# A retention layer and a snake MLP on one core: another written-out order for the first three blocks

## The chip, the cores and the metric

The kernel runs on one core of a Trainium2 chip. The metric is the device time of one execution in microseconds; the times shown are medians of several runs.

## What is computed

The reference, cut to what matters:

```
scores = scale * q @ k.T                              # q, k, v: (8 batches, 8 heads, 576, 64)
ret    = scores * D      # D[i,j] = gamma_h ** (i-j) for i >= j, else 0
x      = (ret @ v), heads side by side                # (4608, 512)
h      = x @ w_in                                     # (512, 2048)
s      = sin(alpha * h)
g      = h + s * s / (alpha + 1e-9)
out    = g @ w_out                                    # (2048, 512) -> (4608, 512) float32
```

Everything comes as float32; the kernel rounds the operands of the matmuls to float16.

## The kernel before

**Tiling.** The 4608 rows are worked as nine blocks of 512 rows. Blocks 0 to 7 are the first 512 rows of each batch; block 8 is the last 64 rows of all eight batches together. In a batch, the 512 rows are two pieces `p` of 256 rows, and the retention is computed in chunks of 128 rows with a carried state `kvs` instead of the full triangle.

**Attention of a batch, `at[b]`.** `load(b, nm, p)` brings one piece of q, k or v as 512 KB on SP's DMA queue into a `raw` buffer (six of them). `cast` scales it by powers of gamma and rounds it to float16, on the engine named: `V` is VectorE (DVE in the profile), `A_` is ScalarE (ACT), `G_` is GpSimd (POOL); `(0,)` or `(1,)` is one half. The transposed form comes from `turn` (eight matmuls on TensorE into a PSUM bank) followed by `take` (a copy out of the bank), or later in the kernel from `crossed` (a transposing DMA on SP's queue). `outer` makes the products of k and v for the state, `take_sum`, `next_sum`, `evict` and `more` bring them out and add them up, `to_state` scales and rounds the state, `scores` and `masked` make `ret`, `values` and `add_states` make the output of the attention, and `keep` copies it as float16 into `xT`.

**The MLP of a block.** `project(n, fc)` is four matmuls of 128x512 that make one of the 16 column groups of `h` in a PSUM bank (with a last argument 0 or 1, only for the first or second 256 rows). `sine` is on ScalarE, `square` on the engine named, `product` on VectorE adds the two and writes `gT`; it is also what gives the PSUM bank back. `gemm2(n, u)` is four matmuls for a quarter of one of the four output tiles, `finish(n, c)` copies the tile out and stores it. The banks have the names `h0`, `h1`, `h2`, `op` (one bank each) and `m0`, `m1` (two banks each).

**Weights.** `load_w_in(g)` and `load_w_out(g)` bring a quarter of each matrix, 1 MB of float32 written as 512 KB of float16, on GpSimd's DMA queue.

**Order.** All work of blocks 0 to 2, with the attention of batches 0 to 4 that goes with it, is written out by hand, one call a line (lines 637 to 1113): each engine executes its instructions in the order of that list, and semaphores come from the tiles that the calls share. From block 3 on (line 1117) a loop over 16 units a block gives the order. `keep_busy` issues matmuls on zeros, so that TensorE has work while data comes. A tile with `bufs=n` goes round n buffers in the order of the requests.

Of the kernel before, what the change touches and what calls it, by code (L numbers as in the profile page):

```python
# [10 lines left out]
F32 = mybir.dt.float32  # L11
F16 = mybir.dt.float16
ADD = mybir.AluOpType.add
MULT = mybir.AluOpType.mult


@with_exitstack
def kernel(
# [86 lines left out]

    raw = {}
# [3 lines left out]
    def load(b, nm, p):  # L110
        if p < 2 and b >= HALVED and nm != "q":
            t_ = work.tile([P, H, 2 * D], F32, tag="raw", bufs=6, name=nm + "32")
# [6 lines left out]
        elif p < 2:  # L119
            t_ = work.tile([P, H, 2 * D], F32, tag="raw", bufs=6, name=nm + "32")  # L120
# [10 lines left out]
    nbuf = {"k": 4, "q": 3, "v": 4}  # L131

    def cast(b, nm, p, eng, ys=(0, 1)):
        t_ = raw[b, nm, p]
        if (b, nm, p) not in half:
            if p < 2:
                d_ = work.tile([P, 16 * D], F16, tag=nm + "16", bufs=nbuf[nm], name=nm + "16")
# [41 lines left out]
    def new_T(b, nm, p):  # L179
        if (b, nm, p) not in T:  # L180
            T[b, nm, p] = (
                work.tile([P, 8, P], F16, tag=nm + "T", bufs=4, name=nm + "T")
                if p < 2
                else work.tile([P, 4, P], F16, tag=nm + "Ts", bufs=B // 2, name=nm + "Ts")
            )
        return T[b, nm, p]
# [54 lines left out]
    class Attention:  # L241
# [11 lines left out]
        def tile(self, name, shape, dtype, bufs):  # L253
            if name not in self.tiles:
                self.tiles[name] = work.tile(shape, dtype, tag=name, bufs=bufs, name=name)
            return self.tiles[name]

        @property
        def x(self):
            xs[self.b] = self.tile("xT", [P, KT, 512], F16, 3)  # L260
            return xs[self.b]

        @property
        def kvs(self):
            return self.tile("kvs", [P, 4, 4, D], F32, 1)

        def state_of(self, c):
            return self.tile("s16", [P, 3, 4, D], F16, 2)[:, c] if c < 3 else sS[:, self.b]
# [56 lines left out]
        def more(self, c):  # L325

            s32 = work.tile([P, 4, D], F32, tag="s32", bufs=2, name="s32")
# [27 lines left out]
        def masked(self, p, y):  # L355
            sc = self.sc.pop((p, y))
            ret = work.tile([P, 2, 512], F16, tag="ret", bufs=4, name="ret")
# [171 lines left out]
    def sine(n, fc):  # L529
        hps = hps_of[n, fc][0]  # L530
        s_t = work.tile([P, 512], F16, tag="s", bufs=4, name="s_t")
# [5 lines left out]
    def square(n, fc, eng):  # L537
        s_t = hps_of[n, fc][1]
        ss_t = work.tile([P, 512], F16, tag="ss", bufs=4, name="ss_t")
# [56 lines left out]

    def make_constants():
# [30 lines left out]
    with tc.manual_schedule():  # L628
# [7 lines left out]

        load(0, "k", 0)
        load(0, "q", 0)
        cast(0, "q", 0, V, (1,))
        cast(0, "k", 0, V, (1,))  # L640
        cast(0, "k", 0, G_, (0,))
        load(0, "v", 0)
        cast(0, "v", 0, A_)
        keep_busy(16, "h0", 256)
        keep_busy(44, "op", 64)
        at[0].outer((0,), "h0", "h1")
        cast(0, "q", 0, V, (0,))
        turn(0, "k", 0, "op")
        turn(0, "q", 0, "h2")
        take(0, "k", 0, V, (0,))  # L650
        at[0].take_sum(0, V)
        take(0, "k", 0, A_, (1,))
        take(0, "q", 0, A_)
        load(0, "q", 1)
        cast(0, "q", 1, G_)
        load_w_in(0)
        load(0, "k", 1)
        cast(0, "k", 1, V)
        load_w_in(2)
        turn(0, "q", 1, "h0")  # L660
        at[0].scores(0, 1, "m0")
        turn(0, "k", 1, "h1")
        at[0].to_state(0, A_)
        take(0, "k", 1, A_)
        load(0, "v", 1)
        at[0].scores(0, 0, "m1")
        turn_alpha()
        take_alpha()
        keep_busy(10, "h2", 256)
        take(0, "q", 1, A_)  # L670
        load(1, "q", 1)
        at[0].take_sum(1, V)
        at[0].more(1)
        at[0].to_state(1, A_)
        cast(0, "v", 1, V)
        at[0].masked(0, 1)
        at[0].masked(0, 0)
        load_w_in(1)
        at[0].outer((1,), "h2", "h1")
        cast(1, "q", 1, G_)  # L680
        at[0].scores(1, 0, "m0")
        turn(1, "q", 1, "op")
        at[0].masked(1, 0)
        at[0].scores(1, 1, "m1")
        at[0].masked(1, 1)
        at[0].take_sum(2, A_)
        at[0].more(2)
        load_w_in(3)
        at[0].to_state(2, G_)
        load_w_out(0)  # L690
# [3 lines left out]
        at[0].values(1, False, "h0", "h2")  # L694
        load(1, "q", 0)
        take(1, "q", 1, A_)
        at[0].values(1, True)
        at[0].add_states(1)
        at[0].keep(0, V)
        project(0, 2, "m1", 0)  # L700
        at[0].keep(1, V, A_)
        project(0, 2, "m1", 1)
        sine(0, 2)
        project(0, 1, "op")
        keep_busy(2, "h0")
        square(0, 2, V)
        invert_alpha()
        product(0, 2)
        cast(1, "q", 0, G_)
        load(1, "v", 0)  # L710
        at[0].next_sum(3)
        sine(0, 1)
        square(0, 1, A_)
        project(0, 0, "h2")
        sine(0, 0)
        cast(1, "v", 0, A_)
        project(0, 8, "h0", 0)
        project(0, 3, "m0")
        sine(0, 3)
        project(0, 8, "h0", 1)  # L720
        product(0, 1)
        square(0, 0, V)
        product(0, 0)
        square(0, 3, G_)
        product(0, 3)
        project(0, 11, "m1")
        load_w_out(1)
        sine(0, 8)
        turn(1, "q", 0, "op")
        take(1, "q", 0, A_, (0,))  # L730
        sine(0, 11)
        take(1, "q", 0, V, (1,))
        project(0, 6, "h1")
        sine(0, 6)
        square(0, 6, V)
        at[0].to_state(3, G_)
        load_w_out(2)
        square(0, 11, A_)
        product(0, 6)
        product(0, 11)  # L740
        project(0, 7, "h2")
# [494 lines left out]
```

## Time and profile before

| | |
|---|---|
| median of 3 runs | 307.27 us (306.55 to 307.67) |
| profiled execution | 306.96 us |
| its span, first to last instruction | 305.2 us |
| mean granted TensorE clock | 0.994 |
| busy: TensorE / VectorE / ScalarE / GpSimd | 293.5 / 204.5 / 182.7 / 136.2 us |
| first `project` (block 0) starts | 20.91 us |
| first `project` of block 1 starts | 50.26 us |
| first `gemm2` of the loop (block 3's stage) | 107.74 us |

In the profile's rows a group is one line of the kernel on one engine; after the count comes the busy time and, in brackets or behind a bar, how long the engine stood idle before it and what it waited for. PEld is the weight load, which runs beside PE. The page's busy time of PE is not a measure of PE at its peak, since matmuls overlap; the distance from one matmul to the next is.

### The profile page before, as it was taken

Reading aid. Unit: us, or ns where it says so; the run is one execution under the profiler, and the core shown is the slowest. Engines: PE = TensorE matmul, PEld = TensorE weight load, DVE = VectorE, ACT = ScalarE, POOL = GpSimd, SP = SyncE. Lnnn points to the kernel's source line nnn. Section 1 sums busy time; section 2 is a strip of 40 time slices with the busy share of each in tenths; the row PEclk is TensorE's granted clock in tenths of the full one; section 3 lists DMA queues with packets and bytes.
Section 4 is the critical chain, followed back from the end, with each engine's and each line's share of the span. In section 5 each row is a group of like instructions: output and inputs, shape, how many; then the busy total and the mean of one; then the engine's idle time right before and its main releaser. Section 6 shows DMA issues by size and latency. Waiting matters only on the chain.

```text
span 305.2 us, 7933 instructions
## 1 busy us (share of the span) xinstructions
PE 293.5 (96%) x3257; PEld 149.6 (49%) x3257; DVE 204.5 (67%) x296; ACT 182.7 (60%) x294; POOL 136.2 (45%) x155
## 2 busy tenths in 40 slices
PE   6879989999999999999999999999999999999995
PEld 5655556455444544454445444544454454444443
DVE  2768988899679796767665777566666746555600
ACT  1649935675365758665677567756764556555411
POOL 4794760498379488578039726653030000000000
PEclk9799999999999999999999999999999999999999
DMA  8999999997695978978689989866441111111132
GB/s 232 338 217 216 216 247 330 242 312 188 166 256 167 167 175 199 255 124 181 146 226 178 170 190 257 161 143 161 105 112 37 34 37 37 35 35 37 46 88 72
DMA packets 115508, 49.85 MB, mean 163 GB/s; under 512 B 69760, under 2 KB 110992, under 8 KB 115472
## 3 DMA queue, kind: packets, MB, share of 16 engines
q1 hardware_dynamic: 110912, 44.97, 62.8%
q0 software_dynamic: 4224, 4.19, 8.1%
q8 instruction: 25, 0.41, 0.6%
q10 hardware_dynamic: 336, 0.18, 0.3%
q14 instruction: 11, 0.09, 0.1%
HBM read 36.75 MB, written 9.44 MB: 151 GB/s over the span
## 4 chain that ended last, share of the span: by engine, by line
PE 82%; DMA 9%; POOL 3%; DVE 2%; ACT 1%; SPq 1%; issue 1%; DVEq 0%; ACTq 0%
PE ops L567 39%; PE hps L524 36%; DMA v<-in_v_dram 7%; PE sc L347 2%; PE o L389 2%; DMA q<-in_q_dram 2%; PE kv L283 1%; POOL q L169 1%; SPq L121 1%; POOL w_in L92 1%; PE o L411 1%; DVE ss_t L543 1%; DVE k L169 0%; DVE ret L359 0%; ACT v L102 0%
## 5 line engine op out<-in xcount | busy, mean ns | idle before, releaser
L567 PE MATMUL ops<-w_out,gT 128*128 128x512 f16 (+2 forms) x592 | 142.4, 373 | 0.9 <-DMA w_out<-in_moe_w_out_dram 0.4
L548 DVE SCALAR_TENSOR_TENSOR gT<-ss_t,inva,hps 128x512 f16<-128x512 f16 x144 | 106.2, 745 | 52.0 <-ACT ss_t L541 45.5
L532 ACT ACTIVATE s_t<-hps,alpha_t 128x512 f16<-128x512 f32 x144 | 97.3, 687 | 70.9 <-PE hps L524 68.1
L524 PE MATMUL hps<-xT,w_in 128*128 128x512 f16 (+1 forms) x544 | 126.5, 367 | 0.3
L524 PEld LDWEIGHTS <-w_in 128*128 128x128 f16 x608 | 58.6, 98 | 64.5 <-DVE xT L104 0.6
L567 PEld LDWEIGHTS <-gT 128*128 128x128 f16 x592 | 56.3, 98 | 65.0 <-issue 1.6
L543 DVE TENSOR_TENSOR ss_t<-s_t 128x512 f16<-128x512 f16 x72 | 43.6, 608 | 19.3 <-ACT s_t L532 18.7
L541 ACT ACTIVATE ss_t<-s_t 128x512 f16<-128x512 f16 x62 | 38.8, 632 | 0.9
L102 ACT COPY osb<-ops 128x512 f32<-128x512 f32 (+1 forms) x34 | 19.7, 582 | 22.0 <-PE ops L567 20.6
L169 POOL TENSOR_TENSOR k<-k,cn 128x1024 f16<-128x1024 f32 (+1 forms) x13 | 22.3, 1712 | 22.1 <-DMA k<-in_k_dram 17.9
L169 POOL TENSOR_TENSOR q<-q,cn 128x1024 f16<-128x1024 f32 (+1 forms) x16 | 27.2, 1710 | 10.9 <-DMA q<-in_q_dram 10.9
L359 DVE TENSOR_TENSOR ret<-sc,mask 128x1024 f16<-128x1024 f32 x20 | 23.9, 1219 | 4.2 <-PE sc L347 4.2
L329 POOL TENSOR_TENSOR kvs<-s,kvs 128x256 f32<-128x256 f32 x22 | 16.2, 734 | 4.0 <-ACT kvs L102 2.3
L543 POOL TENSOR_TENSOR ss_t<-s_t 128x512 f16<-128x512 f16 x10 | 10.8, 1084 | 14.6 <-ACT s_t L532 14.6
L102 ACT CAST xT<-o 128x1024 f16<-128x1024 f32 (+1 forms) x14 | 13.2, 957 | 6.1 <-PE o L411 5.9
L524 PE MATMUL hps<-xS,w_in 128*128 128x512 f16 x64 | 16.4, 379 | 0.0
L153 POOL TENSOR_TENSOR ks<-ks,cn 128x512 f16<-128x512 f32 x4 | 4.2, 1044 | 24.6 <-DMA vs<-in_v_dram 18.1
L104 POOL CAST v<-v 128x1024 f16<-128x1024 f32 (+1 forms) x10 | 10.0, 1007 | 11.1 <-DMA v<-in_v_dram 11.1
L328 POOL TENSOR_TENSOR s<-kvs,cn 128x256 f32<-128x256 f32 x22 | 14.3, 650 | 0.3
L321 POOL TENSOR_TENSOR s<-kvs,cn 128x256 f16<-128x256 f32 x19 | 12.2, 646 | 0.9 <-ACT kvs L102 0.4
L389 PE MATMUL o<-ret,v 64*64 64x128 f16 (+1 forms) x512 | 11.0, 214 | 0.9 <-DVE ret L359 0.4
L359 DVE TENSOR_TENSOR ret<-sc,mask_halved 128x768 f16<-128x768 f32 x12 | 11.4, 950 | 0.0
(62 smaller groups left out, 148.9 us busy)
## 6 DMA issues: line engine op xcount, KB each, us to landing
out_dram<-osb SPq DMA_DIRECT2D x70, 128.0 KB, 2.8
q<-in_q_dram SPq DMA_DIRECT2D x16, 512.0 KB, 5.4
k<-in_k_dram SPq DMA_DIRECT2D x10, 512.0 KB, 5.6
v<-in_v_dram SPq DMA_DIRECT2D x10, 512.0 KB, 6.4
k<-in_k_dram SPq DMA_DIRECT2D x24, 128.0 KB, 3.1
v<-in_v_dram SPq DMA_DIRECT2D x24, 128.0 KB, 3.3
w_in<-in_moe_w_in_dram POOLq DMA_DIRECT2D x4, 512.0 KB, 11.6
w_out<-in_moe_w_out_dram POOLq DMA_DIRECT2D x4, 512.0 KB, 11.5
```

What stands on the lines that cost most here:

```text
L102: eng.copy(d_, s_)
L169: eng.tensor_tensor(dst[:, a0:a1].rearrange("p a r t d -> p t (a r) d"), t_.rearrange("p (t a) x -> p t a x", t=2)[:, :, a0:a1].rearrange( ...
L328: nc.gpsimd.tensor_tensor(s32, self.kvs[:, c - 1], g1.unsqueeze(2).to_broadcast([P, 4, D]), MULT)
L329: nc.gpsimd.tensor_tensor(self.kvs[:, c], s32, self.kvs[:, c], ADD)
L359: nc.vector.tensor_tensor(ret.rearrange("p t (z x) -> p (t z) x", z=2)[:, :, 0:n], sc.rearrange("p t (z x) -> p (t z) x", z=2)[:, :, 0:n], ...
L389: made.append(matmul(o[t][halves(e), c : c + 128].rearrange("p (r i) -> p r i", r=2)[:, :, i0:64], v16[halves(g), 4 * t + 2 * x + e, r, :] ...
L524: matmul(hps_of[n, fc][0][:, cols], w_in16[:, a, fc * P : (fc + 1) * P], xs[n][:, a, cols], start=(a == 0 and part != 1), stop=(a == KT - ...
L532: nc.scalar.activation(s_t, hps, mybir.ActivationFunctionType.Sin, bias=0.0, scale=alpha_t[:, fc : fc + 1],)
L541: nc.scalar.activation(ss_t, s_t, mybir.ActivationFunctionType.Square)
L543: eng.tensor_tensor(ss_t, s_t, s_t, MULT)
L548: nc.vector.scalar_tensor_tensor(gT[n][:, fc, :], ss_t, inva[:, fc : fc + 1], hps, MULT, ADD)
L567: matmul(ops[n, c, cols.start][:, cols], gT[n][:, fk, c * P : (c + 1) * P], w_out16[:, fk, cols], start=(fk == 0), stop=(fk == FC - 1), sk ...
```

## The change

Three things change; what is computed stays the same.

1. The written-out list for blocks 0 to 2 is replaced as a whole. The same loads, projections, second matmuls and attention steps are in it, in another order, with other engines and PSUM banks. Counted in the two lists: squares on VectorE 20 before and 12 after, on ScalarE 18 and 25, on GpSimd 10 and 11; casts (a half counts as one) on VectorE 15 and 9, on GpSimd 21 and 26, on ScalarE 5 and 5. `wait_for_w_out(g)`, a small DMA on SP's queue that reads a quarter of `w_out` and so holds that queue until the quarter is there, is called four times; the function was there before and was not called.
2. Which SBUF buffer a tile gets comes from a table, `BUFFERS`, one digit for each request, and no longer from going round.
3. In the last stage four more small DMAs, `fill_up`, are put on SP's queue.

In the loop, the banks of the projections go round as `h2, h1, h0` where they went `h2, h0, h1`.

```diff
+BUFFERS = {
+    "raw": "012345024135024135043250130124130254103254103254",
+    "k16": "0123012310230123",
+    "q16": "0121021010210210",
+    "v16": "0123012310320132",
...
+}
...
+    def place(tag, shape, dtype):
+        name = tag + next(slot_of[tag])
+        if name not in places:
+            places[name] = work.tile(shape, dtype, tag=name, bufs=1, name=name)
+        return places[name]
...
-            t_ = work.tile([P, H, 2 * D], F32, tag="raw", bufs=6, name=nm + "32")
+            t_ = place("raw", [P, H, 2 * D], F32)
...
+    PAD = 4
+
+    def fill_up():
+        nc.sync.dma_start(gate, w_out16[:, 0, 0:64])
...
-        h, m = cycle(("h2", "h0", "h1")), cycle(("m0", "m1"))
+        h, m = cycle(("h2", "h1", "h0")), cycle(("m0", "m1"))
...
             if n == 7:
+                for i in range(PAD):
+                    at_unit(3 + i, fill_up)
```

The new list from its start to the first projections, one call after the other:

```
load k0; cast k0 V(0), V(1); turn k0 h0; take k0 A_(1), V(0); load q0, v0; cast v0 A_(0)
keep_busy 3 op, 3 h1; load q1; cast q1 V(0); cast v0 G_(1); keep_busy 1 op; outer(0) h1,h2
load k1; cast k1 V; cast q0 G_; turn q0 h0; take q0 A_; take_sum(0) V; next_sum(1)
load_w_in(0); cast q1 G_(1); load v1; load (1,q,0); cast v1 A_; cast (1,q,0) V
turn k1 op; turn q1 h0; take q1 A_; take k1 A_; scores(0,1); outer(1); take_sum(2) A_
to_state(0) G_; load_w_in(2); more(2); masked(0,1); scores(0,0); masked(0,0); load_w_in(1)
turn (1,q,0) h0; take A_; scores(1,1) m0; keep_busy(21, h1, 128); to_state(2) G_; masked(1,1)
scores(1,0); turn_alpha; take_alpha; to_state(1) A_; masked(1,0); take_sum(3) A_
values(0) m0; keep(0) A_; values(1) h1,h0; load (1,q,1); cast (1,q,1) G_; keep(1) A_,V
turn (1,q,1) op; take V(0); load_w_in(3); project(0,2); take A_(1); project 0, 3, 11, 8, 1, 7, 6, 9, 5, ...
```

(`k0` is piece 0 of k of batch 0; `(1,q,1)` is piece 1 of q of batch 1.) In the old list `(1,q,1)` is loaded, cast and turned there too, and `(1,q,0)` is turned among the projections of block 0. Further down, the new list has

```
square(0,2) G_; product; square(0,0) G_; load_w_out(1); ... square(0,11) G_; ... load_w_out(0), load_w_out(2)
... more(3) of batch 0; load_w_out(3); ... project(0,12) op, (0,14) h0, (0,13) m1, (0,15) h2, (0,4) m0, (0,10) h1
take (1,k,0) A_(1); sine(0,10); cast (1,v,0) A_(1); square(0,10) A_; take (1,k,0) A_(0); gemm2(0,4), (0,12), (0,5), (0,13)
wait_for_w_out(0); scores, outer(0) of batch 1; ... gemm2(0,14), (0,6), (0,7); scores(1,1); load (1,v,1); cast (1,v,1) A_; outer(1)
... gemm2(0,15), (0,0), (0,1); values; gemm2(0,2), (0,3); project(1,6), (1,3), (1,9), (1,7), ...
```

so that twelve `gemm2` of block 0 stand ahead of the first `project` of block 1, where the old list has nine; the other four follow later.

More of the change, by code (lines that the diff above doesn't have):

```diff
@@ L679 @@
[L679 to L682, printed above, removed]
-        at[0].masked(1, 0)
[L684 to L690, printed above, removed]
+        at[0].to_state(1, A_)
+        at[0].masked(1, 0)
+        at[0].take_sum(3, A_)
         at[0].values(0, False, "m0")
@@ new lines @@
+        product(1, 0)
+        cast(3, "k", 0, G_)
+        at[2].to_state(3, G_)
+        load(4, "q", 0)
+        crossed(3, 1, "k")
+        load(4, "k", 0)
+        crossed(3, 0, "q")
+        load(4, "v", 1)
+        crossed(3, 0, "k")
+        at[2].scores(0, 0, "m0")
+        at[2].scores(0, 1, "m1")
+        at[2].masked(0, 1)
+        sine(1, 2)
+        square(1, 2, A_)
+        product(1, 2)
+        at[2].masked(0, 0)
+        project(1, 1, "h1")
+        sine(1, 1)
+        gemm2(0, 11, "h0")
@@ L977 @@
[L977 to L988 removed]
+        cast(3, "v", 1, G_)
+        gemm2(1, 0, "h2")
+        gemm2(1, 1, "h2")
+        gemm2(1, 2, "h2")
+        gemm2(1, 3, "h2")
+        load(4, "k", 1)
+        at[3].scores(1, 0, "m0")
```

773 lines of the change are left out of this document (385 added, 388 removed).

## The prediction

> **What bounds the kernel now.** I read the page's first lines, then the busy times by stage, then PE's part of the chain of waits.
>
> ```profile
> PE 293.5 (96%) x3257; PEld 149.6 (49%) x3257; DVE 204.5 (67%) x296; ACT 182.7 (60%) x294; POOL 136.2 (45%) x155
> ...
> 50.30:106.90 56.60, 56.08 (x734) 28.66 (x733) 47.62 (x65) 34.39 (x56) 37.13 (x39) 1.00 0.93 220
> 36.70:50.30 13.60, 12.17 (x262) 6.70 (x261) 12.20 (x21) 6.02 (x12) 7.19 (x9) 1.00 1.17 272
> 20.90:36.70 15.80, 15.69 (x99) 8.79 (x99) 12.74 (x26) 14.35 (x23) 9.43 (x10) 1.00 1.19 216
> 0.00:20.90 20.90, 14.86 (x327) 12.04 (x328) 11.02 (x16) 9.22 (x19) 14.59 (x24) 0.92 1.04 266
> ...
> 92.61 5.18 PE ops L567 x24
> ```
>
> A stage row gives its length, then the busy time of PE, PEld, DVE, ACT, POOL, then clock, DMA share and GB/s. PE is the bound from 20.9 us on. 5.18 us over 24 matmuls is 0.216 us each, so a `project` or `gemm2` of four is 0.863. Whatever DVE, ACT and POOL save is worth nothing unless PE was waiting, and PE's waits are few: 0.1 us idle in the first 15.8, 1.4 in the next 13.6, 0.5 in the 56.6. The loop's first second matmul starts at 107.74 (below), and what is behind it hardly changes. So the change can win at most about 2 us after 20.9 us, plus what it does to the first 20.9 us. There it can also lose.
>
> **The change part by part.** First the head: when does the first projection start?
>
> ```profile
> 7.82 1.04 ACT L102 CAST v<-v 128x1024 f16<-128x1024 f32 x1 [4.55 <-DMA v<-in_v_dram]
> ...
> 9.36 1.90 POOL L169 TENSOR_TENSOR q<-q,cn 128x1024 f16<-128x1024 f32 x1 [3.40 <-DMA q<-in_q_dram]
> ...
> 11.21 1.68 POOL L92 DMA_DIRECT2D w_in<-in_moe_w_in_dram  x2
> ...
> 20.91 2.15 PE L524 MATMUL hps<-xT,w_in 128*128 128x256 f16 x12
> ...
> L104 POOL CAST v<-v 128x512 f16<-128x512 f32 x2 | 1.4, 707 | 0.0
> L169 POOL TENSOR_TENSOR q<-q,cn 128x1024 f16<-128x1024 f32 x12 | 22.9, 1919 | 10.9 <-DMA q<-in_q_dram 10.9
> L359 DVE TENSOR_TENSOR ret<-sc,mask 128x1024 f16<-128x1024 f32 x20 | 23.9, 1219 | 4.2 <-PE sc L347 4.2
> ...
> DMA packets 2062, 1.04 MB, mean 346 GB/s; under 512 B 32, under 2 KB 2062, under 8 KB 2062
> ...
> q1 hardware_dynamic: 553, 0.28, 91.7%
> q0 software_dynamic: 47, 0.05, 28.6%
> ...
> q0 software_dynamic: 432, 0.43, 83.7%
> q1 hardware_dynamic: 432, 0.22, 35.6%
> ```
>
> The DMA rows are of 8 to 11, 14 to 15 and 31 to 34 us. SP's loads (q1) alone run at 346 GB/s, 512 KB in 1.5 us, as the arrivals at 7.82 and 9.36 also show. Once GpSimd's weight queue (q0) moves, the two take packets one for one (432 and 432): SP's queue falls to 0.22 MB in 3 us, 7.15 us a load, the weights to 0.43 MB, 3.65 us a quarter. The weights' 0.05 MB in the second before 15 put their start at 14.65, 3.45 us after the issue at 11.21.
>
> After the change GpSimd casts half of v (0.71 from 7.82) and all of q (1.92) and issues `w_in` at 10.45, so weights move from 13.9. The seventh load, (1,q,0), lands then (7.82 + 4 x 1.5); the eighth, (1,q,1), gets only the shared rate and lands near 21.05 (in the old order it had 0.7 us more at full rate, hence near 18.4). GpSimd reaches its cast at 19.2 (`more` 16.4 to 17.75, an issue of 0.8, a state of 0.65), waits for it, and takes 1.92: 22.95. `turn` of it is queued on PE ahead of `project(0,2)` and takes 0.6. First projection: 23.6, against 20.91: +2.7. Without that wait VectorE sets it: a cast of 1.22 from 13.95, four `masked` of 1.22 to 20.05, `values`, `keep`, `turn`: 21.8. That is the lower bound; if the shared rate begins still earlier, 24.5 is the upper. I take 23.6, since all its terms are rows.
>
> The Trainium skill ("GPSIMD Engine Reference", section 4.1, Engine selection) would keep two-input elementwise work on VectorE, as GpSimd is about twice as slow. In this trace the full cast is 1919 ns on POOL against 1215 on DVE, 1.6 times; by the page's factor that cast would take an estimated 2.43 us and the sum below be 0.5 higher; I keep the row.
>
> Then block 0's projections and block 1's attention:
>
> ```profile
> 22.90 0.59 PE L580 MATMUL idle<-zero 128*128 128x512 f16 x2
> ...
> 26.80 0.61 PE L202 MATMUL tr<-ident,q 128*128 128x128 f16 x8
> ...
> 30.80 2.50 PEld L524 LDWEIGHTS <-w_in 128*128 128x128 f16 x16 [0.44 <-DMA w_in<-in_moe_w_in_dram]
> ...
> 36.66 1.03 PE L567 MATMUL ops<-w_out,gT 128*128 128x512 f16 x4
> ...
> 38.10 1.02 PE L567 MATMUL ops<-w_out,gT 128*128 128x512 f16 x4 [0.42 <-DMA w_out<-in_moe_w_out_dram]
> ...
> 43.48 1.14 ACT L102 CAST v<-v 128x512 f16<-128x512 f32 x2 [2.49 <-DMA v<-in_v_dram]
> ...
> 44.67 0.45 PE L283 MATMUL kv<-v,k 64*64 64x64 f16 x32 [0.67 <-ACT v L102]
> ...
> 50.26 4.50 PE L524 MATMUL hps<-xT,w_in 128*128 128x256 f16 x28
> ...
> L532 ACT ACTIVATE s_t<-hps,alpha_t 128x512 f16<-128x512 f32 x144 | 97.3, 687 | 70.9 <-PE hps L524 68.1
> L548 DVE SCALAR_TENSOR_TENSOR gT<-ss_t,inva,hps 128x512 f16<-128x512 f16 x144 | 106.2, 745 | 52.0 <-ACT ss_t L541 45.5
> L541 ACT ACTIVATE ss_t<-s_t 128x512 f16<-128x512 f16 x62 | 38.8, 632 | 0.9
> L543 POOL TENSOR_TENSOR ss_t<-s_t 128x512 f16<-128x512 f16 x10 | 10.8, 1084 | 14.6 <-ACT s_t L532 14.6
> ```
>
> PE loses from its queue a `turn` (26.80 to 27.24, 0.44), two warm-up matmuls (0.43) and the wait for `w_in` (0.44), for that quarter now lands before it is needed. It gains a wait: ScalarE has 16 sines (11.0), 7 squares (4.4) and copies of 2.4, 17.8 us for 14 us of projections, and bank `m0` for `project(0,4)` comes free only with `product(0,6)`, about 0.5 late, with 0.2 of small ones. -1.3 + 0.7 = -0.6.
>
> From 36.66 to 50.26 the old list does nine `gemm2` (7.77) in 13.60: 5.83 for the rest. In the new one, counted from the first projection, PE does four `gemm2` from 15.2 to 18.65, a `scores`, waits to 19.2 for ScalarE's `take`, ends `outer` at 20.1 (0.45, as at 44.67), a `gemm2` 21.0, a `turn` 21.5, two `gemm2` 23.2, `scores` 23.65, `outer` 24.1, `scores` 24.5, three `gemm2` 27.1, `values` 28.75, two `gemm2` 30.5, and waits for VectorE's `keep` to 30.75: twelve (10.36) in 15.55, 5.2 for the rest: -0.6. Covered in that: v's last piece, held back by the wait on SP for `w_out`, lands about 45.5 (twelve loads and eight quarters fill the DMAs until then) and is needed by `outer` at 23.65 after the first projection, 47.3; the cast of 1.04 just fits. Were the cover gone, each us later is one us.
>
> From there to the loop:
>
> ```profile
> 77.34 0.55 PEld L524 LDWEIGHTS <-w_in 128*128 128x128 f16 x4 [0.59 <-DVE xT L104]
> ...
> 107.74 1.03 PE L567 MATMUL ops<-w_out,gT 128*128 128x512 f16 x4
> ...
> L543 DVE TENSOR_TENSOR ss_t<-s_t x72: 410/426/2099, 23.0 to 286.0; 128x512 f16<-128x512 f16 x72
> ```
>
> Here DVE had 47.6 of 56.6 us, ACT 34.4, POOL 37.1. Counting the new list by the durations above, each gets about 45: VectorE's relief hides behind PE, and ACT and POOL lose their slack. 0.59 us of PE's waits (for VectorE's `keep`) can go; a new one of 0.6 comes where `project(1,15)` waits for bank `op`, which `product(1,2)` gives back behind a `masked`. Two more such places are likely among 40: I take +0.5, with ends -0.8 (all waits go) and +4 (POOL becomes late, below). The buffer table costs nothing where the old owner is done; its ends lie inside these. The four transfers go on SP's queue at units 3 to 6 of the last stage, ahead of stores whose tiles have four buffers; PE and ACT run on, so 0, ends -0.3 and +0.5.
>
> Sum: +2.7 - 0.6 - 0.6 + 0.5 = +2.0 on the profiled execution's 306.96 (span 305.2, 1.76 around it): 309.0. The median 307.27 lies 0.3 above that execution, within the range given. 0.5%, what a measurement can tell here, is 1.5 us: faster below 305.7, slower above 308.8.
>
> **The rivals.** *Faster: the head is not late and the waits go.* If (1,q,1) lands by 19.2, the head costs 21.8 - 20.9 = +0.9. If v's piece also lands by 44.3, PE's waits of 20.9 to 50.3 go (-1.3 and -1.1) and those behind too (-0.8): -2.3, 304.7. For it: VectorE is freed in the stage where it was 90% busy (12.20 of 13.60). Against: the shared DMA rate. It decides at the landing of (1,q,1).
>
> *v's last piece is late.* Head 21.8 as above, but v at 45.5: `outer`, due at 45.45, waits to 46.6. +0.9 - 0.6 - 0.6 + 1.15 + 0.5 = +1.35: 308.3.
>
> *GpSimd becomes the bound in blocks 1 and 2.* Its casts of (3,q,1) and (3,k,1) stand ahead of the state that batch 2's `values` needs; by my count that state is ready 2.5 us early, after 20 us of GpSimd work. Squares on DVE took up to 2099 ns instead of 426 where POOL worked beside; if POOL's work stretches by a fifth, 4 us, batches 2 and 3 each lose 1.5: +2.0 + 3.0 = 312.0.
>
> *The clock falls.*
>
> ```profile
> 6.00:7.00 1.00, 0.49 (x17) 0.47 (x14) 0.58 (x1) 0.00 (x0) 0.00 (x0) 1.00 1.15 347
> 7.00:8.00 1.00, 0.00 (x0) 0.00 (x0) 1.00 (x3) 0.18 (x1) 0.00 (x0) 1.00 1.15 346
> 8.00:9.00 1.00, 0.09 (x7) 0.08 (x10) 0.31 (x1) 0.86 (x1) 0.00 (x0) 0.94 1.15 346
> 9.00:10.00 1.00, 1.00 (x37) 0.94 (x37) 0.00 (x0) 0.00 (x0) 0.64 (x1) 0.50 1.15 348
> ```
>
> 2.4 us without matmuls (6.49 to 8.91) were enough for 0.50. The new wait for (1,q,1) is 1.8 us; if it has the same effect for some 3.4 us of projections, as from 8.9 to 12.3, half of them is lost: +1.7, 310.7. The Trainium skill ("TensorE: Matmul & The Clock Gate", Part 1) names an idle window of about 3.4 us that runs freely; by it 1.8 us would not do, and this rival would be worth nothing; the trace's 2.4 us with the page's free-running window leave it a small chance.
>
> **How the numbers follow.** Forecast 0.34 (307.8 to 310.4: 0.11 same, 0.23 slower); faster rival 0.30 (303.7 to 306.3: 0.26 faster, 0.04 same); late v 0.14, same; GpSimd 0.15 and clock 0.07, slower. Faster 0.26, same 0.29, slower 0.45. The range takes in the faster rival's own value and GpSimd's: 304.6 to 312.2, leaving out about 0.2.
>
> **What would show it.** Right: the weights' queue moves from 14; POOL's cast of (1,q,1) waits for its DMA to about 21; first projection near 23.6; block 1's first projection near 54.3 (50.26 + 2.6 for three more `gemm2` + 1.5); the loop's first second matmul near 109.7. Wrong: a first projection before 22, a state that PE waits for at batch 2's `values`, a clock under 1.00 after 20 us, or a tail that differs.

## The result

The changed kernel is slower: 310.97 us median (309.99 to 313.46, four runs) against 306.96 for the kernel before (the median of four runs beside it), a ratio of 1.0145 (95% interval 1.0121 to 1.0169). That is +4.0 where +2.0 was forecast; the direction and the range were right, the size was not. Medians are over all runs of a kernel; the ratios leave out runs more than 1.5% above its fastest one, which matters for e4_both, where that is four of ten. The profiled execution took 313.46, the slowest of the four, with a span of 311.7; so its losses add up to 6.5 and not to 4.0, and below each of them is held against further profiles.

### The profile page after: what moved, and what is told of

Read it like the earlier page. It is cut to its first block, busy times and chain, and to the rows that moved or that the text cites. A ratio compares the mean times of both kernels' runs of the same rounds, so it can differ in the third digit from the quotient of the medians.

```text
span 311.7 us, 7855 instructions
## 1 busy us (share of the span) xinstructions
PE 293.7 (94%) x3205; PEld 146.9 (47%) x3205; DVE 196.6 (63%) x271; ACT 192.8 (62%) x323; POOL 143.8 (46%) x162
## 3 DMA queue, kind: packets, MB, share of 16 engines
q0 software_dynamic: 4224, 4.19, 8.1%
## 4 chain that ended last, share of the span: by engine, by line
PE 79%; DVE 6%; DMA 6%; POOL 4%; issue 2%; ACT 2%; SPq 1%; ACTq 0%; POOLq 0%; DVEq 0%
PE ops L593 36%; PE hps L550 34%; PE sc L373 3%; DVE gT L574 2%; PE o L415 2%; DMA kT<-k 2%; DMA raw<-in_q_dram 2%; DMA raw<-in_k_dram 2%; POOL k L195 1%; PE tr L228 1%; PE kv L309 1%; DVE ss L569 1%; DVE q L195 1%; POOL v L122 1%; ACT s L558 1%
## 5 line engine op out<-in xcount | busy, mean ns | idle before, releaser
L574 DVE SCALAR_TENSOR_TENSOR gT<-ss,inva,hps 128x512 f16<-128x512 f16 x144 | 106.0, 746 | 56.8 <-ACT ss L567 49.8
L558 ACT ACTIVATE s<-hps,alpha_t 128x512 f16<-128x512 f32 x144 | 97.6, 685 | 65.8 <-PE hps L550 62.7
L569 DVE TENSOR_TENSOR ss<-s 128x512 f16<-128x512 f16 x64 | 37.3, 583 | 19.2 <-ACT s L558 18.6
L567 ACT ACTIVATE ss<-s 128x512 f16<-128x512 f16 x69 | 43.1, 630 | 2.5 <-DVE gT L574 1.4
L195 POOL TENSOR_TENSOR k<-raw,cn 128x1024 f16<-128x1024 f32 (+1 forms) x16 | 26.9, 1689 | 19.5 <-DMA raw<-in_k_dram 19.4
L195 POOL TENSOR_TENSOR q<-raw,cn 128x1024 f16<-128x1024 f32 (+1 forms) x14 | 24.2, 1741 | 2.9 <-DMA raw<-in_q_dram 2.9
L569 POOL TENSOR_TENSOR ss<-s 128x512 f16<-128x512 f16 x11 | 11.4, 1057 | 16.3 <-ACT s L558 16.2
L122 POOL CAST v<-raw 128x1024 f16<-128x1024 f32 (+1 forms) x14 | 14.2, 1016 | 9.9 <-DMA raw<-in_v_dram 9.6
L120 ACT COPY kvs<-kv 128x512 f32<-128x512 f32 (+2 forms) x15 | 8.2, 561 | 10.2 <-PE kv L309 9.0
```

Of the source, the lines that this page charges most:

```text
L120: eng.copy(d_, s_)
L122: eng.tensor_copy(d_, s_)
L195: eng.tensor_tensor(dst[:, a0:a1].rearrange("p a r t d -> p t (a r) d"), t_.rearrange("p (t a) x -> p t a x", t=2)[:, :, a0:a1].rearrange( ...
L558: nc.scalar.activation(s_t, hps, mybir.ActivationFunctionType.Sin, bias=0.0, scale=alpha_t[:, fc : fc + 1],)
L567: nc.scalar.activation(ss_t, s_t, mybir.ActivationFunctionType.Square)
L569: eng.tensor_tensor(ss_t, s_t, s_t, MULT)
```

## The profile after

First the page: span and engines.

```profile
span 311.7 us, 7855 instructions
...
PE 293.7 (94%) x3205; PEld 146.9 (47%) x3205; DVE 196.6 (63%) x271; ACT 192.8 (62%) x323; POOL 143.8 (46%) x162
```

VectorE did 7.9 us less than before, ScalarE 10.1 and GpSimd 7.6 more, and TensorE the same. No engine comes near TensorE's share. What was lost was lost in waits and in TensorE's clock, and the timeline of TensorE shows where (start, duration, operation, and in brackets the idle time before it with what ended it):

```profile
21.85 0.30 PE L415 MATMUL o<-ret,v 64*64 64x128 f16 x7 [1.28 <-issue]
...
23.60 1.68 PE L550 MATMUL hps<-xT,w_in 128*128 128x256 f16 x11
...
36.40 5.31 PE L550 MATMUL hps<-xT,w_in 128*128 128x256 f16 x20 [2.23 <-DVE gT L574]
41.99 1.24 PE L593 MATMUL ops<-w_out,gT 128*128 128x512 f16 x5
...
56.43 3.83 PE L550 MATMUL hps<-xT,w_in 128*128 128x512 f16 x17
...
81.91 0.43 PE L437 MATMUL o<-qT,s 64*64 64x128 f16 x8 [1.74 <-POOL s L347]
82.27 5.14 PE L593 MATMUL ops<-w_out,gT 128*128 128x512 f16 x16
87.76 0.42 PE L373 MATMUL sc<-qT,kT 64*64 64x128 f16 x16 [0.36 <-DMA kT<-k]
...
114.29 1.03 PE L593 MATMUL ops<-w_out,gT 128*128 128x512 f16 x4
```

The first projection is at 23.60 (before 20.91), the first `gemm2` at 41.99 (36.66), block 1's first projection at 56.43 (50.26, or 52.85 with the three more `gemm2` that now stand ahead of it), the loop at 114.29 (107.74). From there to the end it is 197.41 against 197.46: the last stage, its bank order and the four small transfers cost nothing.

Three waits stand out. The first is for a product of block 0, the second for batch 2's state, the third for batch 3's transposed k. Behind the first two the clock fell, as the stages show (length, busy time of PE, PEld, DVE, ACT, POOL, clock, DMA share, GB/s):

```profile
36.00:39.00 3.00, 2.60 (x13) 1.43 (x13) 3.00 (x6) 1.30 (x3) 0.00 (x0) 0.76 1.24 207
39.00:42.00 3.00, 3.00 (x17) 1.41 (x16) 1.81 (x3) 2.47 (x4) 2.33 (x3) 0.67 1.22 238
...
81.00:84.00 3.00, 2.09 (x13) 0.82 (x14) 0.89 (x2) 1.21 (x2) 2.72 (x4) 0.66 0.71 175
84.00:87.00 3.00, 3.00 (x12) 1.25 (x11) 0.00 (x0) 0.00 (x0) 1.59 (x3) 0.77 1.13 276
```

Twice, two slices of 3 us at 0.66 to 0.77 lose up to 1.7 us of clock (an estimate from these rows): (0.24 + 0.33) x 3 and (0.34 + 0.23) x 3.

What ended the wait at 36.40 is seen on VectorE and GpSimd:

```profile
32.75 2.74 DVE L569 TENSOR_TENSOR ss<-s 128x512 f16<-128x512 f16 x1 [0.72 <-ACT s L558]
```

```profile
32.46 0.81 POOL L113 DMA_DIRECT2D w_out<-in_moe_w_out_dram  x1
33.29 1.91 POOL L195 TENSOR_TENSOR k<-raw,cn 128x1024 f16<-128x1024 f32 x1
```

The square of group 9, 0.42 us when alone, took 2.74: it ended 0.29 after GpSimd's cast had ended at 35.20, as though it had only then begun its work. The same is in the head, where two casts of VectorE ended 0.55 and 1.10 after a cast of GpSimd:

```profile
9.43 1.64 DVE L195 TENSOR_TENSOR q<-raw,cn 128x512 f16<-128x512 f32 x1 [1.43 <-DMA raw<-in_q_dram]
10.99 2.57 DVE L195 TENSOR_TENSOR k<-raw,cn 128x1024 f16<-128x1024 f32 x1
...
16.17 4.65 DVE L385 TENSOR_TENSOR ret<-sc,mask 128x1024 f16<-128x1024 f32 x4 [0.17 <-PE sc L373]
```

```profile
8.62 1.90 POOL L195 TENSOR_TENSOR q<-raw,cn 128x1024 f16<-128x1024 f32 x1
...
11.41 1.05 POOL L195 TENSOR_TENSOR q<-raw,cn 128x512 f16<-128x512 f32 x1
...
19.93 1.90 POOL L195 TENSOR_TENSOR q<-raw,cn 128x1024 f16<-128x1024 f32 x1
```

The Trainium skill ("SBUF — State Buffer", section "SBUF: two separate sides") says that VectorE and GpSimd share one pair of ports as an exclusive lock: of a VectorE operation with two inputs in SBUF and a GpSimd operation that reads SBUF, the one that starts second fully blocks. The ends above agree: VectorE's operations end 0.29 to 1.10 us after GpSimd's, and not at a shared pace. The order of the starts does not: by the profile two of the three VectorE operations had begun before GpSimd's cast (32.75 against 33.29, 10.99 against 11.41), and it was still VectorE that waited. Both had begun while GpSimd issued a DMA, ahead of its cast; whether the issue holds the ports too, no run here shows.

SyncE's queue leads to the other two waits:

```profile
52.41 5.94 SPq L586 DMA_DIRECT2D out_dram<-osb  x4
58.45 0.53 SPq L149 DMA_DIRECT2D raw<-in_q_dram  x1
...
68.34 3.35 SPq L218 DMA_TRANSPOSE kT<-k  x1
71.79 1.32 SPq L218 DMA_TRANSPOSE qT<-q  x1
73.16 0.59 SPq L149 DMA_DIRECT2D raw<-in_v_dram  x1
73.85 2.17 SPq L149 DMA_DIRECT2D raw<-in_k_dram  x2
```

The last row is the two pieces of k of batch 3. GpSimd's cast of the first waits 2.05 for it and stands ahead of batch 2's state:

```profile
79.38 1.90 POOL L195 TENSOR_TENSOR k<-raw,cn 128x1024 f16<-128x1024 f32 x1 [2.05 <-DMA raw<-in_k_dram]
```

In the kernel before the same queue issued (3,k,1) at 48.41, and six of block 0's eight stores stood behind all loads of batch 3:

```profile
48.41 1.99 SPq L121 DMA_DIRECT2D k<-in_k_dram  x1
...
65.62 5.52 SPq L560 DMA_DIRECT2D out_dram<-osb  x6
```

So the DMA engines pause where they had been busy. Two slices before (first fence) and after (second), DMA share next to last:

```profile
52.00:57.00 5.00, 5.00 (x29) 2.67 (x28) 4.70 (x8) 4.29 (x8) 2.21 (x2) 1.00 1.32 224
57.00:62.00 5.00, 5.00 (x99) 2.42 (x98) 4.18 (x9) 2.43 (x5) 2.36 (x2) 1.00 1.01 305
```

```profile
52.00:57.00 5.00, 4.91 (x105) 2.69 (x103) 2.96 (x4) 2.30 (x7) 4.92 (x7) 1.00 0.50 136
57.00:62.00 5.00, 5.00 (x25) 2.25 (x23) 3.61 (x5) 4.76 (x9) 4.18 (x4) 1.00 0.60 151
```

## The experiments

My theory after the first reading: three separate losses, namely VectorE held by GpSimd in the head, the same at square (0, 9), and batch 2's state behind a cast whose load is late. The rival: one chain (GpSimd's casts, or SyncE's order of transfers) sets the end, and mending one wait moves TensorE to the next. Every group of runs has runs of the kernel before beside it, whose medians lie at 306.65 to 306.78 (307.17 beside e14 to e16).

**The changed kernel once more, and its waits one at a time**

> The changed kernel once more, for a second profile beside its neighbours. Theory: the added time is three waits of PE (the head, 2.7 us; VectorE's square of block 0, group 9, which stretched to 2.74 us beside GpSimd's cast, 2.2 us; the state of batch 2 behind a cast that waits for its load, 1.7 us), and a clock that falls for 3.4 us after each of the last two (up to 1.9 and 1.7 us). Then this profile shows all three waits in the same places, and its total lies between 309.5 and 313.5, by how often the clock falls. Rival: the waits of the profiled run, the slowest of its four, are chance; then one or two of them are absent here and the time is still near 310.

Measured 309.98, ratio 1.0119 (1.0065 to 1.0173); profiled execution 312.59, span 310.9. All three waits come again, with other sizes:

```profile
35.56 3.86 PE L550 MATMUL hps<-xT,w_in 128*128 128x256 f16 x20 [2.15 <-DVE gT L574]
...
79.17 0.31 PE L437 MATMUL o<-qT,s 64*64 64x128 f16 x8 [1.28 <-POOL s L347]
...
85.02 0.42 PE L373 MATMUL sc<-qT,kT 64*64 64x128 f16 x16 [1.98 <-DMA kT<-k]
```

The state was ready earlier here and k's transpose later; together 3.3 us, against 2.1 in the first profile.

```diff
-        square(0, 9, V)
+        square(0, 9, A_)
```

> One square (block 0, group 9) goes from VectorE to ScalarE. Theory: PE's wait of 2.2 us near 34 us and the fall of the clock behind it go: 1.5 to 3.5 us faster than the changed kernel, 307.5 to 309.5. Rival: the products were late for another reason (ScalarE has the most work there, 17.8 us for 14 us of projections), and the wait stays or moves to the next bank: within 0.7 us of the changed kernel.

Measured 309.19, ratio 1.0074 (1.0047 to 1.0101). The wait for the product is 0.52, the first `gemm2` is at 37.98 instead of 39.70, block 1's first projection at 52.43, ahead of the kernel before. From the first projection to the first `gemm2` it is 15.29 instead of 16.93: that this square, on VectorE beside GpSimd's cast, cost 1.6 us of this stage is shown. The time moved the same way, but 309.19 against 309.98 is within the spread of the two. The state and k's transpose are waited for as before:

```profile
78.47 0.31 PE L437 MATMUL o<-qT,s 64*64 64x128 f16 x8 [1.50 <-POOL s L347]
...
83.17 0.42 PE L373 MATMUL sc<-qT,kT 64*64 64x128 f16 x16 [0.83 <-DMA kT<-k]
```

```diff
-        cast(3, "k", 1, G_)
         at[2].to_state(2, G_)
+        cast(3, "k", 1, G_)
```

> The state of batch 2 that PE waits for is made by GpSimd ahead of the cast of (3,k,1) and no longer behind it. Theory: PE's wait of 1.7 us near 80 us and the clock's fall behind it go: 1.5 to 3.5 us faster than the changed kernel, 307.5 to 309.5. Rival: the cast, then the transposing DMA of k, are late instead, and PE waits at the scores of batch 3: within 0.7 us of the changed kernel.

Measured 310.36, ratio 1.0110 (1.0076 to 1.0144). The wait for the state is gone, and the next one has taken its place:

```profile
84.58 0.42 PE L373 MATMUL sc<-qT,kT 64*64 64x128 f16 x16 [2.50 <-DMA kT<-k]
```

So the state's wait, though real, was not what the time hung on.

Both edits together:

> Both edits. Theory: they add up, 3 to 7 us faster than the changed kernel, 304.5 to 308, so that what is left of the loss is the head (2.7 us) less what the new list gains between 42 and 56 us (1.7 us): about 1 us above the kernel before, 306 to 308. Rival: PE's waits move on; over 309.

Measured 308.65, ratio 1.0034 (1.0014 to 1.0055), ten runs from 306.60 to 313.92: between the theory and the rival. The profiled run was one of the long ones, 312.91. In it the wait for the state is gone and that for the product is 0.52, but TensorE waits 4.16 for batch 3's transposed k: the waits moved on, as the rival had it.

**The head**

```diff
+        cast(0, "q", 0, V)
...
-        cast(0, "q", 1, V, (0,))
+        cast(0, "q", 1, V)
...
+        for _ in range(5):
+            nc.gpsimd.memset(filler, 0.0)
...
-        cast(0, "q", 0, G_)
...
-        cast(0, "q", 1, G_, (1,))
```

> The changed kernel with the casts of batch 0's q on VectorE alone; GpSimd fills their place with five memsets of a small tile, so that the weight transfers start when they did. Theory: VectorE's casts of q and k of piece 1 took 1.64 and 2.57 us where 0.69 and 1.22 are usual because GpSimd's casts ran beside them; without those they take the usual time, VectorE's line of casts and masks ends about 1 us earlier, and the first projection starts near 21.8 (22.8 to 23.6 in the two profiles of the changed kernel). Rival: (1,q,1), which shares the DMAs with the weights, or PE's own issue sets the start: it stays at 22.7 or later.

One run, on the changed kernel: 308.86. VectorE's cast of k is short again although it has two more halves to do, and the first projection starts at 22.00:

```profile
11.09 1.23 DVE L195 TENSOR_TENSOR k<-raw,cn 128x1024 f16<-128x1024 f32 x1 [0.58 <-DMA raw<-in_k_dram]
```

That the casts are held by GpSimd's is shown by this 1.23 against 2.57. What it is worth, the same edit on e8_loads (below) says:

> e8_loads with the head of e5_head as well: block 0's q casts on VectorE, GpSimd filled with memsets for the same stretch. Theory (VectorE's two-input casts are held while a two-input cast runs on GpSimd, and the first projection pays for it): the casts of q and k take 0.7 and 1.2 us instead of 1.6 and 2.6, the first projection starts at about 22.0 instead of 23.0, block 1's at about 51.8 instead of 52.6, and the time is e8_loads' 307.8 less 0.8, so 307.0. Rival (the later transposes are the bound): batch 2's second scores still start at about 73.3, the wait of TensorE for the q transpose there grows from 1.8 to about 2.6, and the time stays at 307.8.

Measured 308.18, ratio 1.0053 (1.0031 to 1.0076), not under e8_loads' 307.77. The first projection came at 22.81, against 23.00 in e8_loads, and batch 2's second scores at 72.95, against 73.30, behind a wait of 1.25. The time is the rival's, but not for its reason: the wait did not grow, the head had gained only 0.2 to give back. So the held casts are shown, and that they delay the first projection by more than 0.2 is not: it varies from 22.0 to 24.1 among all profiles of the new list. Why so little was gained is on VectorE's row of e10_headload. VectorE is done with what stands ahead at 13.91, but its cast of (1,q,0) waits for its load to 14.42 and then takes 1.73 beside an operation of GpSimd, so that the masks start at 16.07, against 15.91 in e8_loads. That load was nearly as late as the casts had been.

**GpSimd's load, or the order of transfers**

Block 1's squares (7) and (13) from GpSimd to VectorE and (5) and (4) to ScalarE, on e4_both:

> The kernel of the two edits (square of group 9 on ScalarE, state of batch 2 earlier), and the four squares of block 1 that were given to GpSimd go to VectorE and ScalarE, two each. Theory: GpSimd's 4.2 us of squares stand ahead of the cast of (2,q,1), SP's queue waits with the transposes for that cast, and the load of (3,k,1) waits behind the transposes, so PE's wait for the transposed k of batch 3 (4.2 us) shrinks by 2 to 4 us: 305 to 307. Rival: the load's place in SP's order sets it, whatever GpSimd does: within 0.8 us of 308.65.

Measured 308.84, ratio 1.0070 (1.0043 to 1.0098): no faster than e4_both with 4.2 us less on GpSimd. Its profile has a wait of 1.27 for the transposed k, and three new ones of 0.46 to 0.57 for VectorE and ScalarE; with the 4.16 of e4_both's long execution that can't be compared.

On e4_both, the load of (3,k,1) is moved ahead of batch 2's second transposes, and (4,v,0) behind (3,k,0); three digits of the buffer table change places so that the slot is free:

```diff
+        load(3, "k", 1)
         crossed(2, 1, "k")
         crossed(2, 1, "q")
-        load(4, "v", 0)
-        load(3, "k", 1)
         load(3, "k", 0)
+        load(4, "v", 0)
```

> The kernel of the two edits, and on SP's queue the load of (3,k,1) goes ahead of the two transposes of batch 2's piece 1, the load of (4,v,0) behind those of k. Theory as above, that SP's order is what delays k: the load is issued about 5 us earlier, GpSimd's cast no longer waits, PE's wait for the transposed k shrinks by 2 to 3 us: 305.5 to 307. Rival: GpSimd's own line of work is what is late; the cast moves by less than 1 us and the time stays within 0.8 us of 308.65.

Measured 307.77, ratio 1.0044 (1.0017 to 1.0071). Both of the waits are gone. The one ahead of them has grown from 0.81 in e2_sq9, since batch 2's transposes now run behind a load:

```profile
73.30 0.64 PE L373 MATMUL sc<-qT,kT 64*64 64x128 f16 x32 [1.80 <-DMA qT<-q]
```

Both edits:

> Both of these together. Theory (GpSimd's line and SP's order form one chain): the wait for k is gone, the loop is reached at 107.3 to 108, 304.5 to 306.5, level with the kernel before or a little better. Rival: another wait takes its place: over 307.5.

Measured 308.02, ratio 1.0045 (1.0030 to 1.0060). The four squares make no difference to the time with the loads in order either. In the profile they do: the wait for q is 0.93 instead of 1.80, but two waits of 0.39 and 0.64 for products are new, behind the squares that VectorE has taken over. So giving these squares away gains nothing, whereas moving loads took away both waits; whether GpSimd's quantity of work would count if VectorE had room for the squares is not shown.

Next the transposes ahead of the loads, on e10_headload:

> e10_headload with batch 2's second transposes (crossed(2, 1, k) and crossed(2, 1, q)) moved ahead of the loads (3, q, 1), (3, v, 0) and (3, k, 1) on SyncE. Theory (SyncE's order sets what is late in block 1): the transposes issue at about 63 to 67 instead of 65.8 to 71, the wait of TensorE for q ahead of batch 2's second scores (1.8 in e8_loads) is gone, the loop starts 1.5 to 2 us earlier and the time is 305.5, under the kernel before's 306.7. Rival (the loads that are now behind are as much needed): the casts of batch 3 on GpSimd wait for their loads again, batch 2's state or batch 3's k transpose comes late by as much, and the time stays at 307 or over.

Measured 312.11, ratio 1.0185 (1.0159 to 1.0212). The wait for q is gone, as the theory said; but the load of (3,v,0) went out at 67.62 instead of 63.93, GpSimd's cast of it ran at 72.36 instead of 69.17, and TensorE waited for k's transpose:

```profile
84.18 0.42 PE L373 MATMUL sc<-qT,kT 64*64 64x128 f16 x16 [3.30 <-DMA kT<-k]
```

The loads are as much needed as the transposes: the rival is right, and the order among them only chooses which is late. Only the k transpose moved forward, to a place before that, on e8_loads and on e9_sqld:

> e8_loads with one step moved: batch 2's second k transpose, crossed(2, 1, k), is issued ahead of crossed(2, 0, k), where its data lie ready and SyncE's queue has a pause, and no longer behind the loads (3, v, 0) and (3, k, 1). The loads keep their places, unlike in e11_cross. Theory (what remains of the loss is SyncE's order alone): the q transpose behind it issues at about 67 instead of 69.8, TensorE's wait of 1.8 for it goes, the load (3, k, 0) goes out 2 to 3 us earlier, batch 3's k transpose is no later than TensorE, the loop starts 1.0 to 1.8 earlier than in e8_loads and the time is 306.3, level with the kernel before (306.7). Rival (GpSimd is the bound behind it): the wait moves to batch 2's state or batch 3's k transpose, and the time stays at 307.5 to 308.

> The same move made in e9_sqld, where four of block 1's squares have been taken off GpSimd. SyncE theory: as in e12_kfirst, the 0.9 us wait for the q transpose goes, but the waits of 0.4 and 0.6 for products behind VectorE's squares stay: 307.2. Rival (GpSimd's squares are what makes the casts of batch 2 and 3 late): this is the faster of the two, 306.2 or less, and e12_kfirst stays at 307.5 or over.

Measured 308.31, ratio 1.0060 (1.0037 to 1.0083), and 309.64, 1.0088 (1.0056 to 1.0121): neither better than what it was made from, and both theories failed; in e12_kfirst a wait of 0.90 for batch 3's transposed k came up, as its rival had said. The q transpose was issued 2.9 earlier in e12_kfirst, as expected, but it now held SyncE for 3.17 us, and TensorE waited 1.40 for it.

**The pause of the transfers**

What was left to try is the pause of the transfers from 52 to 62 us itself. In a first attempt four loads of batch 3 went ahead of the stores of `finish(0, 1)`:

> e8_loads with four loads of batch 3, (3, q, 0), (3, v, 1), (3, q, 1) and (3, v, 0), issued ahead of the stores of finish(0, 1). Theory (the loss that is left is one of transfers: while SyncE's queue stands at those stores, 49 to 55 us, no load goes out, the DMA share falls to half, and the loads of batch 3 then meet the transposes of batch 2): the DMA share rises over 1.0 in 52 to 57 us and falls behind it, GpSimd's cast of (3, v, 0) no longer waits for its load, the q transpose that TensorE waited 1.8 for comes 1 us or more earlier, and the time is 306.3 to 306.8, level with the kernel before. Rival (the loads wait for their slots on SyncE and hold up stores and transposes instead): batch 2's first k transpose issues after 58, waits for bank or k transposes of 1 us or more appear, and the time is 308.5 or over.

> e12_kfirst with the same four loads ahead of finish(0, 1). Theory of the transfers: with the loads out of the way the early k transpose takes 1.3 us on SyncE instead of 2 or more, both of TensorE's waits of e12_kfirst (1.4 and 0.9) are gone or under 0.5, the time is 305.8 to 306.3, under the kernel before. Rival: as in e14_early, 308.5 or over.

> The changed kernel with the four loads ahead of finish(0, 1), nothing else. The loads (4, v, 0) and (3, k, 1) still stand behind batch 2's second transposes. Theory of the transfers: these transposes end earlier, so (3, k, 1) is issued at about 69 instead of 71.6 to 73.9, the waits for batch 2's state and batch 3's k transpose shrink by 2 us together, 308.5. Rival (only the place of (3, k, 1) counts): 310, with the two waits as before.

These three decide nothing: (3,q,1) and (3,v,0) were loaded over two pieces of batch 2 that came to be cast after them, so batch 2's casts read, and waited for, batch 3's data. They took 316.22, 315.79 and 317.44.

Then each load behind the last cast of the piece whose slot it takes:

```diff
+        load(3, "q", 0)
+        load(3, "v", 1)
         finish(0, 1)
...
         cast(2, "q", 0, V)
+        load(3, "q", 1)
+        load(3, "v", 0)
...
         finish(0, 0)
-        load(3, "q", 0)
-        load(3, "v", 1)
```

(The old places of (3,q,1) and (3,v,0), further down, are empty too.) Alone in the changed kernel:

> The changed kernel with the same four loads moved, nothing else. (4, v, 0) and (3, k, 1) still stand behind batch 2's second transposes. Theory of the transfers: these transposes end earlier, (3, k, 1) is issued about 2 us earlier than 71.6 to 73.9, the waits for batch 2's state and batch 3's k transpose shrink by 2 us together: 308.5. Rival (only the place of (3, k, 1) in the list counts): 310, with the two waits as before.

Measured 309.07, ratio 1.0076 (1.0049 to 1.0104). Of the waits for state and k's transpose, 2.1 and 3.3 us in the two profiles of the changed kernel, 0.55 is left, though (3,k,1) stands where it stood in the list. From block 1's first projection to the loop it is 54.53, against 57.86 and 59.21. Square (0, 9) is untouched and costs as much as ever:

```profile
36.58 5.25 PE L550 MATMUL hps<-xT,w_in 128*128 128x256 f16 x20 [2.22 <-DVE gT L574]
...
80.76 0.31 PE L437 MATMUL o<-qT,s 64*64 64x128 f16 x8 [0.55 <-POOL s L347]
```

But the pause was not filled, and (3,k,1) went out 0.8 us earlier than in the first profile, not 2:

```profile
52.00:57.00 5.00, 4.91 (x105) 2.70 (x104) 2.96 (x4) 2.30 (x8) 4.92 (x7) 1.00 0.40 115
```

```profile
69.67 1.32 SPq L218 DMA_TRANSPOSE kT<-k  x1
71.10 1.25 SPq L218 DMA_TRANSPOSE qT<-q  x1
72.40 0.59 SPq L149 DMA_DIRECT2D raw<-in_v_dram  x1
73.09 1.94 SPq L149 DMA_DIRECT2D raw<-in_k_dram  x2
```

The first of the four loads, now ahead of the stores, waited 5.1 us for GpSimd's cast of the piece that had its slot, so the DMA share of 52 to 57 us is no higher than before (0.40 against 0.50). What did move are the two last: (3,q,1) went out at 58.72 instead of 66.37, (3,v,0) at 59.19 instead of 67.70. GpSimd's cast of (3,v,0) no longer waits (71.01, in the first profile 73.31 behind a wait of 2.36), the k transpose takes 1.32 instead of 3.35, the cast of (3,k,1) starts 1.3 earlier, and the state is ready 1.2 earlier. From block 1's first projection up to that state TensorE's timeline is the same in both profiles within 0.15 us.

With e8_loads' edits:

> e8_loads with four loads of batch 3 issued earlier on SyncE: (3, q, 0) and (3, v, 1) ahead of the stores of finish(0, 1), (3, q, 1) and (3, v, 0) ahead of those of finish(0, 0), each behind the last cast of the piece that had its slot. Theory (what is left of the loss is a pause of the transfers while SyncE's queue stands at these stores): the DMA share rises to over 1.0 in 52 to 57 us, GpSimd's cast of (3, v, 0) finds its load there, the q transpose that TensorE waited 1.8 for comes 1 us or more earlier, and the time is 306.3 to 306.8, level with the kernel before. Rival (the loads stand on SyncE for their slots and hold up stores and transposes instead): batch 2's first k transpose issues later than 57.5, waits of 1 us or more appear for banks or for k transposes, and the time is 308.5 or over.

Measured 307.47, ratio 1.0028 (1.0006 to 1.0050), the best of the new list; the profiled execution took 306.73, span 304.7, against 306.96 and 305.2 before. The DMA share in 52 to 57 us is 1.06 against 0.68 in e8_loads, the cast of (3,v,0) finds its data and runs at 66.83 (69.76 in e8_loads, behind a wait of 2.61), and q's wait is halved:

```profile
52.00:57.00 5.00, 5.00 (x25) 2.29 (x24) 3.71 (x5) 4.75 (x11) 4.16 (x4) 1.00 1.06 303
```

```profile
66.83 0.61 POOL L122 CAST v<-raw 128x512 f16<-128x512 f32 x1
```

```profile
72.11 0.64 PE L373 MATMUL sc<-qT,kT 64*64 64x128 f16 x32 [0.87 <-DMA qT<-q]
```

The same with e12_kfirst:

> e12_kfirst with the same four loads moved as in e17_early. Theory of the transfers: with the loads out of the way the early k transpose and the q transpose behind it take 1.3 to 2 us on SyncE instead of 2 to 3, the two waits of e12_kfirst (1.4 and 0.9) are under 0.5, and the time is 305.8 to 306.3, under the kernel before. Rival: as in e17_early, 308.5 or over.

Measured 308.49, ratio 1.0055 (1.0030 to 1.0079): a wait of 1.32 for q is left of the 1.40 and 0.90, and the time is no better than e12_kfirst's 308.31. The k transpose brought forward is no gain here either.

So it is shown that the place of batch 3's loads on SyncE's queue makes these waits: two different moves on that queue, of (3,k,1) in e8_loads and of four other loads in e19_early_only, each take them away or nearly so. That the pause of the transfers as such does it is not shown, since e19_early_only has the pause and hardly the waits. In the times the four loads are worth 0.9 to 1.9 us alone (309.07 against 309.98 and 310.97, of which only the second is clear of the spread); between e8_loads and e17_early, 0.3 us apart, the intervals overlap, and between e12_kfirst and e18_early_k nothing is gained. No version of the new list beats the kernel before.

## Why the prediction missed, step by step

The stages as they were summed, in us against the kernel before, from the starts of the first projection, the first `gemm2`, block 1's first projection and the loop in each profiled execution (2.59 are taken off for the three `gemm2` that moved):

| stage | predicted | after | e1_again | e2_sq9 | e17_early |
|---|---|---|---|---|---|
| head | +2.7 | +2.69 | +1.86 | +1.78 | +1.83 |
| block 0's projections | -0.6 | +2.64 | +1.18 | -0.46 | -0.56 |
| first `gemm2` to block 1 | -0.6 | -1.75 | -1.74 | -1.74 | -1.75 |
| block 1 to the loop | +0.5 | +2.97 | +4.32 | +2.38 | -0.16 |
| loop to the end | 0 | -0.05 | +0.08 | -0.06 | +0.14 |
| sum | +2.0 | +6.5 | +5.7 | +1.9 | -0.5 |

Two terms failed, block 0's projections and the way from block 1 to the loop; the third term was 1.1 wrong the other way, which hides a part of that in the sum.

*Head.* The number was met, once exactly, by luck: the reason was wrong. The piece (1,q,1) did not land at 21.05: GpSimd's cast of it ran at 19.93 and waited for no DMA. I had let the weights move from 13.9 and slow SyncE's queue down from there. They began about a microsecond later, and while SyncE's queue still had most of the engines; by 16 us it had moved 4.19 MB, its first eight pieces of 512 KB with (1,q,1) as the last:

```profile
q1 hardware_dynamic: 595, 0.30, 99.3%
q0 software_dynamic: 31, 0.03, 18.9%
```

(Packets, MB and share of the DMA engines, of 14 to 15 us.) What the projection waited for was VectorE's chain, which stood as the lower bound at 21.8: the masks run from 16.17 to 20.82 and not to 20.05. The casts of 1.64 and 2.57, instead of 0.69 and 1.22, are ahead of them, but without these the load of (1,q,0) held the masks up as long (e10_headload). Behind the masks TensorE stood idle for another 1.03 us in the first profile (to 21.85, `issue`: for nothing that the profile shows) and for 0.20 in e1_again; no term held that, and it is the whole difference between 23.60 and 22.77. I had quoted a VectorE operation stretched to 2099 ns beside GpSimd and used it only for a rival.

*Block 0's projections.* This term failed: -0.6 was forecast, +1.2 and +2.6 measured. It had a price for ScalarE's work and for bank `m0`, but none for a VectorE square held up beside a cast of GpSimd. -0.6 is right where square (0, 9) is off VectorE (e2_sq9, -0.46). In the changed kernel the held square cost 1.6 in e1_again and, with the clock's fall behind it, 3.1 in the first profile.

*First `gemm2` to block 1.* The sign was right and the gain 1.1 larger: about the faster rival's share for v. ScalarE's cast of v's last piece ran at 48.01 and waited for no DMA, so v did come early enough.

*From there to the loop.* This term failed as well: +0.5 was forecast, +2.4 to +4.3 measured. I counted the engines' work, 45 us each, and found it to fit; but not SyncE's queue, on which four stores and the first transposes now stood ahead of batch 3's loads. With four of these loads issued earlier and nothing else changed the stage is at -0.4 (e19_early_only: 54.53 us, with the 2.59 of the moved `gemm2` 57.12, against 57.48 before). The rival with GpSimd as the bound named the right mark (batch 2's state) and a size near the truth, but not the cause: it let GpSimd's work stretch, while GpSimd's casts waited 2.36 and 2.05 for their loads.

*Clock.* The rival of a falling clock was placed in the head, behind a wait for (1,q,1) that did not exist. The clock did fall, behind other waits: 2.23 and 1.74 in the first profile, 2.22 in e19_early_only, where those 20 matmuls took 5.25 us instead of 3.86. The Trainium skill ("TensorE: Matmul & The Clock Gate", Part 1), by whose idle window of some 3.4 us I had kept this rival small, does not agree with that. It is not a matter of length alone either: behind 2.15 us in e1_again the projections kept full speed.

*Tail, four transfers.* Nothing, as predicted (-0.05). What the buffer table costs ahead of the loop was not measured by itself.

What stays open: e17_early's median is 0.8 above the kernel before while its profiled execution is 0.2 below; its runs spread from 306.47 to 309.95, with one of 314.91 beyond, those of before from 306.21 to 307.70. Its head is 1.8 us late and made good by block 1's first projection, which may leave less slack for what follows; this is argued, and which wait varies from run to run, one profile a kernel can't say. Nor do these runs say how the +4.0 of the medians is shared out: the stages are known for one execution of a kernel each.

## What to carry to other kernels

Where an order is written out by hand, go through the DMA queue as a list of its own: a store waits for the end of a chain of work, and every load behind it waits too, though its own buffer may be free by then (here (3,q,1) and (3,v,0) could go out 7.7 and 8.5 us earlier). Put loads whose slots are free ahead of stores, and no others: three kernels here took a slot too early. When two-input work is moved from VectorE to GpSimd, price two-input work that is left on VectorE beside it as ending when GpSimd's operation ends, on the chain that TensorE waits for; and when a wait is taken away, look at once for what is late next, since three of the edits here only changed the name of the wait.

## What was not expected of the hardware

A transposing DMA occupied SyncE's queue for 1.25 to 1.36 us where no load had just been issued (e11_cross, 63.61 and 65.07) and for up to 3.90 where two had (e8_loads, 65.77); in e12_kfirst the q transpose went out 2.9 us earlier than in e8_loads and ended only 1.0 earlier. And in one execution a TensorE wait of 1.74 us was enough for the clock to fall: the 16 second matmuls behind it took 5.14 us, where behind waits of 1.28 and 1.50 they took 3.63.
